# A new order for the 1,205 tasks of a block-causal attention and channel-mix kernel

## The chip, the core and the metric

The kernel runs on one core of a Trainium2 chip. The metric is the device time of one execution in microseconds (us). The kernel before the change took 271.82 us as the median of three runs (270.72 to 274.71). One further execution was taken with the hardware profiler; every time below that isn't called a median comes from it.

The core's engines run side by side, each through its own instructions in order: TensorE (PE, with its weight loads as PEld), VectorE (DVE), ScalarE (ACT), GpSimd (POOL) and SyncE (SP), whose instructions here only issue transfers. Transfers themselves are carried out by 16 DMA engines.

## What is computed

Attention over 8 batches of 8 heads, 576 positions, head size 64, with a mask by blocks of 64 positions; the result, x, with 512 columns, goes through a channel mix with squared relu and a sigmoid gate:

```python
scores = scale * np.matmul(q, k.transpose(0, 1, 3, 2))
scores = np.where(block_i >= block_j, scores, -1000000000.0)
attn = softmax(scores);  x = attn @ v            # heads side by side: 8 x 576 x 512
x_prev = x shifted by one position
xk = mu_k * x + (1.0 - mu_k) * x_prev
xr = mu_r * x + (1.0 - mu_r) * x_prev
k = np.maximum(xk @ w_k, 0.0)                    # 512 -> 1024
v = k * k @ w_v                                  # 1024 -> 512
r = 1.0 / (1.0 + np.exp(-(xr @ w_r)))            # 512 -> 512
out = r * v
```

Inputs and output are float32; the products run in bfloat16 (q, k) and float16.

## The kernel before

**Tasks.** The program makes a list of 1,205 tasks. A task is a short function that issues a few instructions of one engine. A table of numbers, `ORDER`, says in which order the tasks are issued; since every engine works through its instructions in the order of issue, the table fixes the order on each engine and in SP's queue of transfers. A number with a plus sign (`0+12`) also puts that many *spare matmuls* in front of the task (function `unread`, line 279): products of an identity matrix into a tile that nobody reads. A second table, `PLACE`, has one letter (P, D, A) for each task that may run on more than one engine: POOL, DVE or ACT.

**Buffers.** Tiles come from rings of a few buffers (line 180): 8 buffers `ld` for raw loads of q, k and weights, 4 `vl` for raw v, 4 `nb` and 8 `nl` for q and k in bfloat16, 2 `qkt` for transposed q and k, 13 `e` for exponentials, 3 `s` and 2 `mm` in PSUM. A task that takes a buffer waits until the last reader of what was there before is done. The buffer is chosen in `Plan.issue`, so a new order also gives new buffers.

**Tasks of attention**, for batch b and head pair:

- `longld` (batches 0 to 3, line 251): q or k of a head pair, rows of 2,304 bytes; `long` casts it (lines 262, 268); `qt` transposes it on PE (18 small products, line 371), `ev` copies it out of PSUM.
- `qkld` and `tlld` (batches 4 to 7, line 251): the same data in pieces of 256 bytes, two issues each; `qk` and `tail` cast it; `turn` (line 318) transposes a pair by a DMA transpose into `qkt`. In this text "turn 6 0" is that of batch 6, pair 0.
- `vld` (line 251): a piece of v; `v` casts it.
- `sc` (lines 489, 499): a group of score products; `ex` its exponential on ACT (line 517). "sc 6 01" is batch 6, group 0, block set 1; it needs the turns of pairs 0 and 2, and "sc 6 15" those of pairs 1 and 3.
- `av` S, T, A, B (lines 554, 577, 586): sums and products with v; `t1`, `rec`, `t2`, `norm` on DVE divide by the sums.

**Tasks of the channel mix**, for nine chunks c of 512 rows (batch and chunk borders differ: chunk 8 is batch 7's rows alone, chunk 7 has rows of batches 6 and 7): `d` and `mul` mix neighbouring positions (lines 739, 742, 766, 770); `pk` is xk @ w_k, eight tasks of four products each (line 794), `relu` (804, 806) and `sq` (812, 814) follow; `pr` is xr @ w_r (line 828), `tanh` follows (836); `pv` is the product with w_v, eight products (line 854), `o` combines (864), `store` writes 256 KB to the output (line 872). Weights come by `wld` (line 251) and are cast by `w`.

**What sets the order.** The core is the walk through the table:

```python
        for word in ORDER.split():
            n, _, fill = word.partition("+")
            t = self.tasks[int(n)]
            t["fill"] = int(fill or 0)
            out.append(t)
```

SP's queue holds every load, turn and store of the kernel. An instruction there that waits (a load for its buffer, a turn for its casts, a store for its output) holds all that stand behind it.

Of the kernel before, what the change touches and what calls it, by code (L numbers as in the profile page):

```python
# [14 lines left out]
LONGS = 4  # L15

ORDER = """
# [66 lines left out]
"""  # L84

PLACE = (
    "DAPAPPPPDPPDAPAPAPAPPPAPPAAADDAADDDAADDDDPPPDDPDDDDDPPPDDPPDDPPPPD"
    "PDPPPAPDAADDDDDPAPDPPAPDAAPAPADDADDADAAPPDPDPDDPDPAPPPAAADAADAAPPP"
    "ADDDDDPPADPPPDPPPDDDPPDADADDAAAPPPDDDPPPDDPPPDADPPPAPPPPDPDDPDDPDP"
    "APDDDPDAPDADADAAPDAADDDAADPADAAAPDADPDDADDPAAAADAAAAPADAAAPAPAAAAA"  # L90
    "DAAADAPAPADAPAAAAAAADAPDDAAAAAPAPAPADAAADAAAAAPADAPAAAPADDPAPADADA"
    "PAPAPADADADDAAPAPADADADADAP")


class Plan:
# [868 lines left out]
```

## Time and profile before

| | |
|---|---|
| median of three runs | 271.82 us (270.72 to 274.71) |
| profiled execution: device time | 270.97 us |
| profiled execution: span, first to last instruction | 269.2 us |
| PE busy (3,700 matmuls) | 247.1 us, 92% |
| DVE, ACT, POOL busy | 196.7, 184.8, 92.3 us |
| mean granted clock of PE | 0.987 |
| share of the 16 DMA engines that data transfers took | 75.5% |
| DMA packets under 512 bytes | 98,816 of 110,249 |
| stores after 198 us | 17 of 37 |

Device time is 1.8 us more than the span: what lies around the first and last instruction. Matmuls are pipelined, so their busy time overlaps and a busy PE isn't a PE at its peak; a group's rate is read from the starts of neighbouring groups. The share of DMA engines is that of time in which they held packets.

### The profile page before, as it was taken

The numbers are of one execution on the slowest core, as the hardware profiler recorded it, in microseconds if no ns is written. First come the engines' busy times: TensorE is split into PE (matmuls) and PEld (weight loads), VectorE is DVE, ScalarE is ACT, GpSimd is POOL, SyncE is SP. The second block draws the span as 40 slices with busy tenths as digits, with TensorE's granted clock in tenths as the row PEclk, the third lists the DMA queues.
The fourth block names the chain that finished last, engine by engine and source line by source line (L and its number), as shares of the span: only waits on it lengthen the run. The fifth ranks groups of instructions, "written<-read, shape, count | busy, mean of one in ns | idle before, by whom it ended". The sixth has DMA issues, their size and how long they took to land.

```text
span 269.2 us, 8792 instructions
## 1 busy us (share of the span) xinstructions
PE 247.1 (92%) x3700; PEld 123.4 (46%) x3700; DVE 196.7 (73%) x354; ACT 184.8 (69%) x270; POOL 92.3 (34%) x123
## 2 busy tenths in 40 slices
PE   7879779899899996789899999699999999999995
PEld 3544336444446444334354445345444544444442
DVE  1597696999888976266968969588985599943432
ACT  4869588788786885399569886695788563661440
POOL 3555614731337311365155103413403350140310
PEclk9988799999999999999999999999999999999999
DMA  7999997899999697998999899889932201202213
GB/s 217 391 205 315 268 228 209 261 259 228 220 239 223 166 226 162 207 209 225 201 198 225 195 223 207 199 192 219 194 104 78 80 4 39 80 0 79 78 56 144
DMA packets 110249, 48.83 MB, mean 181 GB/s; under 512 B 98816, under 2 KB 99072, under 8 KB 110208
## 3 DMA queue, kind: packets, MB, share of 16 engines
q1 hardware_dynamic: 110208, 48.25, 75.5%
q8 instruction: 29, 0.48, 0.8%
q14 instruction: 12, 0.10, 0.1%
HBM read 33.56 MB, written 9.44 MB: 160 GB/s over the span
## 4 chain that ended last, share of the span: by engine, by line
PE 62%; DMA 13%; DVE 8%; ACT 7%; SPq 4%; issue 3%; POOL 1%; DVEq 0%; ACTq 0%; POOLq 0%
PE t_mm L854 18%; PE t_mm L794 15%; PE t_mm L828 10%; PE t_s L489 5%; PE t_s L586 5%; DMA t_vl<-in_v_dram 4%; ACT t_e L517 4%; SPq L251 4%; DMA out_dram<-t_o 2%; DMA t_ld<-in_q_dram 2%; PE t_s L577 2%; DMA t_qkt<-t_nb 2%; PE t_s L371 2%; DMA t_ld<-in_k_dram 2%; ACT t_kr L804 2%
## 5 line engine op out<-in xcount | busy, mean ns | idle before, releaser
L517 ACT ACTIVATE t_e<-t_s 128x1024 f16<-128x1024 f32 (+1 forms) x96 | 88.9, 977 | 15.4 <-PE t_s L489 13.4
L794 PE MATMUL t_mm<-t_xk,WK 128*128 128x512 f16 x288 | 67.8, 379 | 4.1 <-ACT t_kr L804 2.7
L854 PE MATMUL t_mm<-WV,t_k 128*128 128x512 f16 (+1 forms) x296 | 66.4, 374 | 0.2 <-DVE t_k L814 0.2
L804 ACT ACTIVATE t_kr<-t_mm 128x512 f32<-128x512 f32 x61 | 36.2, 599 | 29.2 <-PE t_mm L794 23.1
L814 POOL TENSOR_TENSOR t_k<-t_kr 128x512 f16<-128x512 f32 x26 | 29.0, 1128 | 60.5 <-ACT t_kr L804 36.8
L794 PEld LDWEIGHTS <-WK 128*128 128x128 f16 x288 | 26.7, 97 | 37.0 <-issue 8.2
L854 PEld LDWEIGHTS <-t_k 128*128 128x128 f16 x296 | 27.7, 98 | 33.8 <-issue 2.3
L864 DVE SCALAR_TENSOR_TENSOR t_o<-t_t,t_mm 128x512 f32<-128x512 f32 (+1 forms) x37 | 24.8, 670 | 20.4 <-PE t_mm L854 13.0
L828 PE MATMUL t_mm<-WR,t_xr 128*128 128x512 f16 x144 | 35.9, 379 | 0.7 <-ACT t_kr L804 0.7
L770 DVE SCALAR_TENSOR_TENSOR t_xk<-t_d,MUK,t_xt 128x384 f16<-128x384 f32 (+7 forms) x56 | 30.8, 563 | 7.2 <-POOL t_d L742 7.2
L770 DVE SCALAR_TENSOR_TENSOR t_xr<-t_d,MUR,t_xt 128x384 f16<-128x384 f32 (+7 forms) x56 | 32.7, 599 | 0.0
L836 ACT ACTIVATE t_t<-t_mm 128x512 f32<-128x512 f32 x36 | 21.4, 598 | 16.1 <-PE t_mm L828 13.3
L489 PE MATMUL t_s<-t_qkt 64*64 64x64 bf16 (+7 forms) x560 | 25.4, 291 | 3.3 <-DMA t_qkt<-t_nb 3.3
L742 POOL TENSOR_TENSOR t_d<-t_xt 128x576 f32<-128x576 f32 x16 | 19.0, 1193 | 23.7 <-DVE t_xk L770 12.0
L814 DVE TENSOR_TENSOR t_k<-t_kr 128x512 f16<-128x512 f32 x24 | 18.1, 755 | 8.5 <-ACT t_kr L804 8.4
L586 PE MATMUL t_s<-t_e,t_vo 64*32 64x64 f16 (+7 forms) x1120 | 20.8, 284 | 1.1 <-POOL t_vo L268 1.1
L828 PEld LDWEIGHTS <-t_xr 128*128 128x128 f16 x144 | 13.5, 97 | 17.8 <-issue 3.0
L489 PEld LDWEIGHTS <-t_qkt 64*64 64x64 bf16 x560 | 12.4, 106 | 17.5 <-issue 10.2
L268 POOL CAST t_vo<-t_vl 128x576 f16<-128x576 f32 (+1 forms) x17 | 12.9, 761 | 20.9 <-DMA t_vl<-in_v_dram 20.9
L586 PEld LDWEIGHTS <-t_vo 64*32 64x32 f16 x1120 | 14.6, 92 | 9.1 <-issue 3.2
L268 DVE COPY t_qkt<-t_s 128x576 bf16<-128x576 bf16 x18 | 13.1, 752 | 7.3 <-PE t_s L371 6.6
L268 POOL CAST t_nl<-t_ld 128x576 bf16<-128x576 f32 x18 | 11.8, 666 | 19.0 <-DMA t_ld<-in_k_dram 13.4
(73 smaller groups left out, 242.5 us busy)
## 6 DMA issues: line engine op xcount, KB each, us to landing
out_dram<-t_o SPq DMA_DIRECT2D x35, 256.0 KB, 2.9
t_vl<-in_v_dram SPq DMA_DIRECT2D x56, 144.0 KB, 4.2
t_ld<-in_q_dram SPq DMA_DIRECT2D x16, 288.0 KB, 5.5
t_ld<-in_k_dram SPq DMA_DIRECT2D x16, 288.0 KB, 5.3
t_ld<-in_q_dram SPq DMA_DIRECT2D x32, 128.0 KB, 3.5
t_ld<-in_k_dram SPq DMA_DIRECT2D x32, 128.0 KB, 3.7
t_ld<-in_moe_w_k_dram SPq DMA_DIRECT2D x8, 256.0 KB, 6.0
t_ld<-in_moe_w_v_dram SPq DMA_DIRECT2D x8, 256.0 KB, 4.0
```

The source lines that it names most:

```text
L268: e.tensor_copy(dst, src)
L489: nc.tensor.matmul(PS[y * D:y * D + D, x, col:col + n], kq[:, 1, t * D:t * D + D], kq[:, 0, q0:q0 + n], start=True, stop=True)
L517: nc.scalar.activation(new(ebuf)[:, :, 0:w], new(m)[:, :, 0:w], AF.Exp, scale=ISQ)
L586: nc.tensor.matmul(PA[out, u, HALF + f * D:HALF + f * D + D] if kind == "T" else PA[out, u, lo - D:lo - D + n], weight((b, rows, c, t % JT ...
L770: nc.vector.scalar_tensor_tensor(dst, dt[:, 0, lo:lo + w], (MUK1, MUR1)[n][:, cc:cc + 1], x, ALU.mult, ALU.add)
L794: nc.tensor.matmul(ps, WK[:, cc, jc * P:(jc + 1) * P], new(tiles["xkb", c])[:, cc], start=(cc == 0), stop=(cc == CCn - 1))
L804: nc.scalar.activation(kt, ps, AF.Relu)
L814: (nc.vector if eng == "DVE" else nc.gpsimd).tensor_tensor(dst, KR, KR, ALU.mult)
L828: nc.tensor.matmul(ps, xr[:, cc, jt * P:(jt + 1) * P], WR[:, cc], start=(cc == 0), stop=(cc == CCn - 1))
L836: nc.scalar.activation(new(tb), new(m), AF.Tanh, scale=0.5)
L854: nc.tensor.matmul(ps[:, 0:w], k2[:, jc, jt * P:(jt + 1) * P], WV[:, jc, cols], start=(jc == 0), stop=(jc == JCn - 1))
L864: nc.vector.scalar_tensor_tensor(new(o)[:, 0:w], new(tiles["tbf", c, jt])[:, cols], 1.0, new(m)[:, 0:w], ALU.add, ALU.mult)
```

## The change

Only the two tables change. The tasks, their dependencies and the rings stay. The change's own description is: same tasks in a new order; the plan that wrote the tables now counts waits inside transfer issues, SyncE's instruction fetches, and TensorE's instruction blocks behind transfers. The planner isn't in the program; what can be seen is the new order:

```diff
 ORDER = """
-5 6 0+12 9 10 3 7 73 75 76 13 74 4 8 69+1 17 14 113 70 18 88 71 114 72 179
-81+1 89 15 83 11 181 97 98 109 12 16 84 82 110 177 178 100+4 101 182 121 122
...
+11 0+12 7 8 5 12 77 15 78 6 71 72 16 73+7 74 79 3 4 80 9 69+1 70 91 17 18 10
+13 173 174 92 75 169 76 177 178 109+4 14 113+1 88+4 110 114 89 100 97+6 85
...
 PLACE = (
-    "DAPAPPPPDPPDAPAPAPAPPPAPPAAADDAADDDAADDDDPPPDDPDDDDDPPPDDPPDDPPPPD"
...
+    "PPDDADPPPPDDDDPAPDPPPAAPADAADAADAAAADAAADDPPDDDPDDPPDDDDPDDDDDPADDP"
...
```

What differs when the tables are read out:

| | before | after |
|---|---|---|
| spare matmuls | 32 | 80 |
| last task with spares, its place in the order | `av 1 2 S`, 202 | `qt 2 0 0 1`, 195 |
| `relu` on ACT, DVE | 61, 11 | 53, 19 |
| `sq` on ACT, DVE, POOL | 22, 24, 26 | 31, 20, 21 |
| `d` on ACT, DVE, POOL | 4, 12, 16 | 4, 17, 11 |
| `qk` on ACT, DVE, POOL | 5, 15, 12 | 6, 11, 15 |
| `v` on ACT, DVE, POOL | 7, 9, 17 | 4, 13, 16 |
| first three transfers on SP | q, k of batch 0 pair 1 and q of pair 0 | q of pair 2, k of pair 0, q of pair 1 |
| `qkld` / `store` / `turn` ahead of turn 6 1 on SP | 26 / 16 / 11 | 32 / 16 / 11 |
| transfer at which the last v piece is loaded | `vld 7 1`, behind turn 7 0 | `vld 7 0`, behind turn 7 1 and three stores of chunks 4 and 5 |
| `pk` whose products PE does first | `pk 0 4` | `pk 0 0` |

The order differs on every engine from the start to the end; the number of transfers, their sizes and the products are the same.

More of the change, by code (lines that the diff above doesn't have):

```diff
@@ L17 @@
 ORDER = """
[66 rows of a table removed]
[66 rows of a table added]
 """
 PLACE = (
-    "DAPAPPPPDPPDAPAPAPAPPPAPPAAADDAADDDAADDDDPPPDDPDDDDDPPPDDPPDDPPPPD"
[L88 to L92, printed above, removed]
+    "PPDDADPPPDDDDPAPDPPPAAPADAADAADAAAADAAADDPPDDDPDDPPDDDDPDDDDDPADDP"
+    "DDAPPDPAAAADDDDPDDPPPAPPPAPDPAPDADDDAAADPPPPPADPPAPDAADADDADDDADDD"
+    "DDDPDPPDPDPPPPPDPDDADDPAPPDPDDAAPDPPPPDPDPAPPDPPDDADDPDPPAAPDDPPPP"
+    "DAPPADAADDPPAPPAPADAAAAAAADAPDPAAAADPAADPDAAPAAAADPADAAAPAPDDAAAPA"
+    "ADPADAAAPAAAAAAAPAPAPADAAAAAADPAPDAAADPDPDAADAADDDAAAAADAAADAADADA"
+    "DADADADAPAAAPADDAADADDDADDD")
 class Plan:
```

128 rows, old and new, of the table ORDER are left out of this document.

## The prediction

> **What bounds the kernel now.** I read the page's busy table first, then a table by stretch, then the chain.
>
> ```profile
> span 269.2 us, 8792 instructions
> ...
> PE 247.1 (92%) x3700; PEld 123.4 (46%) x3700; DVE 196.7 (73%) x354; ACT 184.8 (69%) x270; POOL 92.3 (34%) x123
> ...
> q1 hardware_dynamic: 110208, 48.25, 75.5%
> q8 instruction: 29, 0.48, 0.8%
> ```
>
> PE at 92% looks like the bound, but 75.5% of 16 DMA engines is 203 us, and it isn't spread evenly. The table by stretch (us; busy time and count of PE, PEld, DVE, ACT, POOL; granted clock; DMA share; GB/s) shows where:
>
> ```profile
> 18.40:21.80 3.40, 3.24 (x56) 1.71 (x55) 2.08 (x7) 2.50 (x4) 1.46 (x4) 0.50 0.94 229
> ...
> 28.70:32.10 3.40, 3.40 (x95) 1.81 (x96) 2.88 (x6) 1.33 (x2) 2.92 (x5) 0.50 1.02 221
> ...
> 42.00:60.00 18.00, 16.80 (x309) 8.78 (x302) 17.23 (x29) 14.63 (x26) 9.29 (x10) 1.00 0.83 248
> 60.00:100.00 40.00, 38.16 (x627) 19.22 (x626) 35.30 (x64) 32.04 (x47) 13.34 (x16) 1.00 1.02 217
> 100.00:170.30 70.30, 61.74 (x942) 30.24 (x940) 49.71 (x86) 49.90 (x76) 24.05 (x30) 1.00 0.98 203
> 170.30:198.00 27.70, 27.64 (x474) 13.86 (x475) 24.52 (x42) 21.51 (x32) 9.62 (x11) 1.00 0.99 211
> 198.00:269.20 71.20, 68.05 (x568) 31.89 (x566) 43.08 (x71) 35.96 (x55) 15.57 (x14) 1.00 0.16 61
> ```
>
> From 60 to 198 us the DMA engines are full (0.98 to 1.02); from 170.3 on PE doesn't pause (27.64 of 27.70, then until its last matmul at 266.05). So transfers set the pace to 170, PE after. The chain shows the handover:
>
> ```profile
> 164.27 0.63 SPq L872
> ...
> 165.02 5.30 DMA t_qkt<-t_nb
> 170.32 0.04 issue
> 170.36 0.41 PE t_s L489 x4
> ```
>
> That is turn 6 0 landing at 170.32; sc 6 01 had waited 2.1 us for it. The end is therefore: landing of the last transpose that PE waits for, plus PE's remaining work, plus 3.1 us from the last matmul to the end of the span.
>
> **Two sums, used for both orders.** First, transfers. The trace's packets by size take 21.8 ns (256 B), 97 ns (2,048 B) and 111 ns (2,304 B); over 16 engines a long load is 0.89 us, a qkld or tlld 1.40, a vld 1.57 (batch 0: 1.40, its short one 0.70), a weight or store 0.78, a turn 1.74. Added in SP's order this gives each transfer a position. The landing of each transfer in the trace minus its position is 2.0 us at 21.6 us, 4.7 at 42, 9.1 at 60, then 8.2 to 11.9 with 10.3 at turn 6 0 (position 160.0): one full stream from 60 us on, which had lost time before that. Second, PE's work: starts of neighbouring groups are 0.86 us apart for pk and pr (four 512-column matmuls, 379 ns each but pipelined), 1.73 for pv, 1.32 for av A or B, 1.36 for av S, about 0.24 for a score group, 0.22 for one spare matmul. Ahead of sc 6 01 these make 138.8, behind it 94.7; the trace took 95.7 (170.36 to 266.05).
>
> **The change, part by part.** No transfer or product is removed. (1) *Spare matmuls*, 32 become 80: 48 x 0.216 = 10.4 us of PE, the last of them in qt 2 0 0 1, where PE's sum is 36.5 us, 17.3 of it spares. I cost them at nothing: in the old order PE came to its first pk at 42.07 us with a sum of 28.0, so 14 us were idle or slow, and in the new one the sum ahead of the first pk is 37.6, which leaves 4.4 for start-up and waits to arrive as early. ACT has more ahead as well: its tasks up to batch 1's last exp come to 33.2 us by row means, 28.6 before. If that cover is gone, they delay casts, and so loads.
> The two 0.50 rows above are 6.8 us at half clock; running them at full would save PE 3.4 us. The Trainium skill (TensorE: Matmul & The Clock Gate, Part 1) says that an idle window of about 3.4 us puts the clock at half; by it the spares could win those 3.4 us of PE time, while my sum takes 0, since PE then waits for transfers anyway.
> (2) *Engine places*. By row means DVE gains about 6.7 us (8 more relus at 0.69, 5 more differences at 0.79, 4 fewer squares at 0.76 and others), ACT 1, POOL loses 12. Before, DVE was busy 67.6 of the last 98.9 us; its work behind the binding point is 63.8 us after and 66.5 before. Hidden under PE: 0.
> (3) *Order of transfers*, which decides. PE's first wait for each transpose, as position minus PE's sum ahead of it, was greatest at sc 6 01 and equal within 0.5 at the next three (sc 6 11, sc 7 15, sc 7 03): position plus work behind is 254.5 to 255.0. In the new order the greatest is at sc 6 15, which needs turn 6 1: position 171.7, PE work behind 89.1, together 260.8 (the next: sc 5 12 258.4). Ahead of it stand six more qkld (all of batch 7), two more stores and one more turn than ahead of turn 6 0 before: 6 x 1.395 + 2 x 0.776 + 1.745 = 11.7 us. PE has two pr, one pv, one av and four score groups fewer left: 1.7 + 1.7 + 1.3 + 0.9 = 5.6. With an equally full stream the end moves by 11.7 - 5.6 = **+6.0 us**.
> (4) *Waits inside the early issues*. Between 42 and 55 us SP stood still for buffers of the load ring:
>
> ```profile
> SPq L251 <- ACT t_nl L262: 2.8, 1, 2.8
> SPq L251 <- ACT WV L264: 2.0, 1, 2.0
> SPq L251 <- ACT WR L262: 1.8, 1, 1.8
> SPq L251 <- POOL t_nl L268: 1.4, 1, 1.4
> ```
>
> 8 us of standing cost the stream 4.4 (4.7 to 9.1). The new order takes loads whose buffers come free earlier against PE's non-spare work, but its spares eat part of that: the tightest loads there stand 7 to 9 us behind the PE sum they depend on, 11 to 13 before. So the gain lies between 0 and 4.4; with nothing nearer to either end I take half, **-2.2**.
> (5) *Stores in SP's queue*. A store that waits for its output holds every later load and turn. From 60 to 196 us SP's gaps between issues are 0.04 to 0.4 us, so none did. Ahead of turn 6 1 the tightest are store 3 1 0 (position 149.6, 19.3 us ahead of its PE sum) and store 2 3 0 (17.9); before, 15.7 to 16.3 at positions 69 to 88 was enough. Cost 0, up to 2 us. Behind turn 6 1 store 4 3 0 and turn 7 3 will hold SP a few us, but the later transposes have 7.6 us in hand (253.1 against 260.8).
> (6) *Instruction blocks*. PE's 29 fetches of 16 KB (q8, 0.8%) stay 29 or 30. "issue" is 3.5% of the chain, 9.4 us, fetches in it. Between 0 and 9.4 won; where PE waits for a transpose anyway it is nothing: 0.
> The Trainium skill (DMA: Bandwidth & Descriptors, Queues, rings and completion order) says that each engine takes turns between queue rows packet by packet. By that rule a fetch, on its own row, waits for a packet and not for the queued loads, and planning round it wins 0; if it did wait for the backlog, up to 9.4 us would be won. The q8 packets take 1.1 us each in the trace, against 4.2 from issue to landing for a vld, which agrees with the rule.
>
> **Sum.** Turn 6 1 lands at 170.3 + 11.7 - 2.2 = 179.8; PE's rest is 89.1 x 95.7 / 94.7 = 90.0; the tail 3.1: span 273.0, against 269.2. The profiled run took 270.97, 1.8 over its span: 274.8. The median of the runs before is 0.85 above it (271.82, runs from 270.72 to 274.71): **275.5**.
>
> **Rivals.**
> A, the forecast: 275.5, +1.4%. Chance 0.42.
> B, the stream loses nothing between 42 and 60 us, or nothing after 21 us (10.3 falls to 5.9 or even 2): 273.3 to 269.4. For: the change moves just these loads. Against: spares push PE's sum up. Chance 0.18, within 2%.
> C, slower: the spares. Casts on ACT stand behind exps that wait for PE; if PE comes to its first pk later than about 47 us (42.07 before), the load ring stays full longer than before, and each us more is one for the stream until 182 us. No gain gives 277.7; with 2 to 4 us more lost 280 to 282. For: 7 to 9 us of distance instead of 11 to 13. Against: the idle 14 us. It is the case that ends over 2% slower. Chance 0.32.
> D, the change wins what it says: PE's idle time until 170 us is fetches and blocked issues more than transfers, and their 9.4 us go: 262. For: issue's 3.5%. Against: DMA at 1.00 from 60 us. Chance 0.08, the only case over 2% faster.
>
> **Numbers.** Two per cent, 5.4 us, is about what a measurement of this kernel can tell (its runs span 4). Within 2%: A and B, 0.60; slower 0.32; faster 0.08. The range reaches from B's lower end into C's upper one, leaving out D and the worst of C: 269.5 to 281.5.
>
> **What will show it.** The new chain should hand over from a DMA on t_qkt to PE near 180 us, with PE unbroken behind it for 90 us; DMA share near 1.0 from 60 us; in 42 to 60 us a share above 0.83 (A, B) or below (C). First pk near 43 us says that the spares were covered. Half-clock rows should be fewer. I'm wrong if PE pauses after the handover for DVE or ACT, if a store holds SP ahead of turn 6 1, or if the prices per transfer change with the order.

## The result

The changed kernel takes 274.14 us as the median of 20 runs (270.00 to 278.23), the kernel before, beside it on the same chip, 271.81 (266.96 to 274.90). The ratio is **1.0136, 95% interval 1.0098 to 1.0175**: slower, by 1.4%, a difference under 2% that 20 runs tell from none. (The ratio leaves out executions that took over 1.5% more than the fastest of their kernel; the medians don't, so their quotient is smaller.) The forecast was 275.5, range 269.5 to 281.5.

The profiled execution took 274.5 us, its span 272.4; before, 270.97 and 269.2. The same lines of the page as before:

```profile
span 272.4 us, 8894 instructions
...
PE 255.1 (94%) x3748; PEld 124.8 (46%) x3748; DVE 200.1 (73%) x364; ACT 185.9 (68%) x271; POOL 83.0 (30%) x112
...
q1 hardware_dynamic: 110208, 48.25, 72.3%
q8 instruction: 29, 0.48, 0.8%
```

PE is busier by 8 us, with 48 more spare matmuls in it; the transfers are the same 110,208 packets. The table by stretch of the new kernel (busy us and count of PE, PEld, DVE, ACT, POOL; granted clock; DMA share; GB/s):

```profile
0.00:18.40 18.40, 17.01 (x207) 7.30 (x207) 5.58 (x19) 11.73 (x15) 7.12 (x22) 1.00 0.96 302
18.40:42.00 23.60, 21.95 (x500) 11.16 (x503) 18.63 (x48) 19.65 (x25) 8.18 (x13) 1.00 1.00 249
42.00:60.00 18.00, 18.00 (x472) 10.53 (x457) 17.89 (x31) 16.36 (x30) 8.79 (x11) 1.00 0.96 289
60.00:100.00 40.00, 37.87 (x579) 18.53 (x579) 32.90 (x60) 30.37 (x44) 15.49 (x19) 1.00 0.91 217
100.00:170.30 70.30, 63.79 (x985) 31.35 (x985) 54.92 (x94) 50.63 (x74) 26.68 (x30) 0.98 0.99 205
170.30:182.00 11.70, 9.18 (x125) 4.11 (x123) 7.99 (x15) 7.03 (x11) 3.09 (x5) 1.00 0.61 127
182.00:198.00 16.00, 16.00 (x244) 7.82 (x243) 13.24 (x23) 11.72 (x17) 3.89 (x4) 1.00 0.93 186
```

Two readings carry the rest. In 42 to 60 us the DMA engines now have a share of 0.96, where it was 0.83: the stream loses under 1 us there (landing minus position), where it lost 4.4. SP's waits (41 to 61 us) are shorter, not gone: 7.9 us in all, the longest 1.6, against 9.7 and 2.8. And PE's last pause, in 170.30:182.00, ends at 177.68, 7.3 us later than the old kernel's (170.36); from there on PE is unbroken. From 60 to 100 us the share is 0.91, not near 1.0 as forecast, while 217 GB/s move as before, when it was 1.02: a share near 1 by itself doesn't say that no more could be moved.

The chain of the new kernel at that place (start, us, what):

```profile
171.65 4.16 DMA t_ld<-in_q_dram
...
176.02 0.06 POOL t_nb L268
176.07 0.51 issue
176.59 1.05 POOL t_k L814
...
177.68 1.25 PE t_mm L854 x5
178.94 0.86 PE t_mm L828 x4
179.80 0.62 PE t_s L489 x20
```

The handover to PE is not a DMA on `t_qkt`, as forecast. It is qkld 7 1 0 landing, its cast on POOL, then a square on POOL, then pv 4 3 0 on PE. Turn 6 1 had landed at 177.98; PE came to sc 6 15, which needs it, only at 179.89, 1.9 us later. POOL's timeline in the new kernel (start, busy; in brackets the idle time ahead and what ended it) shows the square waiting behind a cast that had nothing to cast yet:

```profile
168.81 1.35 POOL L742 TENSOR_TENSOR t_d<-t_xt 128x576 f32<-128x576 f32 x1
176.02 0.61 POOL L268 CAST t_nb<-t_ld 128x512 bf16<-128x512 f32 x1 [5.86 <-DMA t_ld<-in_q_dram]
176.59 1.04 POOL L814 TENSOR_TENSOR t_k<-t_kr 128x512 f16<-128x512 f32 x1
```

### The profile page after: what moved, and what is told of

The parts are those of the page before. It is cut to its first block, busy times and chain, and to the rows that moved or that the text cites. A ratio compares the mean times of both kernels' runs of the same rounds, so it can differ in the third digit from the quotient of the medians.

```text
span 272.4 us, 8894 instructions
## 1 busy us (share of the span) xinstructions
PE 255.1 (94%) x3748; PEld 124.8 (46%) x3748; DVE 200.1 (73%) x364; ACT 185.9 (68%) x271; POOL 83.0 (30%) x112
## 2 busy tenths in 40 slices
DMA packets 110248, 48.82 MB, mean 179 GB/s; under 512 B 98816, under 2 KB 99072, under 8 KB 110208
## 3 DMA queue, kind: packets, MB, share of 16 engines
q1 hardware_dynamic: 110208, 48.25, 72.3%
## 4 chain that ended last, share of the span: by engine, by line
PE 69%; DVE 15%; DMA 8%; issue 3%; POOL 1%; ACT 1%; SPq 1%; POOLq 0%; DVEq 0%; ACTq 0%
PE t_mm L794 19%; PE t_mm L854 17%; PE t_mm L828 8%; PE t_mm L279 6%; PE t_s L586 5%; PE t_s L489 5%; DMA t_qkt<-t_nb 3%; PE t_s L577 3%; DMA t_ld<-in_q_dram 3%; DVE t_xr L770 3%; PE t_s L371 2%; DVE t_xk L770 2%; DVE t_d L742 2%; DVE t_xt L650 2%; DVE t_o L864 2%
## 5 line engine op out<-in xcount | busy, mean ns | idle before, releaser
L804 ACT ACTIVATE t_kr<-t_mm 128x512 f32<-128x512 f32 x53 | 31.6, 599 | 25.5 <-PE t_mm L794 25.5
L814 POOL TENSOR_TENSOR t_k<-t_kr 128x512 f16<-128x512 f32 x21 | 22.8, 1093 | 52.1 <-ACT t_kr L804 42.3
L770 DVE SCALAR_TENSOR_TENSOR t_xk<-t_d,MUK,t_xt 128x384 f16<-128x384 f32 (+7 forms) x56 | 33.3, 609 | 1.8 <-POOL t_d L742 1.7
L489 PE MATMUL t_s<-t_qkt 64*64 64x512 bf16 (+7 forms) x560 | 25.3, 291 | 5.2 <-DMA t_qkt<-t_nb 5.2
L742 POOL TENSOR_TENSOR t_d<-t_xt 128x576 f32<-128x576 f32 x11 | 13.3, 1213 | 42.5 <-DVE t_xt L642 20.6
L812 ACT ACTIVATE t_k<-t_kr 128x512 f16<-128x512 f32 x31 | 18.7, 635 | 6.5 <-PE t_mm L854 4.5
L806 DVE TENSOR_SCALAR t_kr<-t_mm 128x512 f32<-128x512 f32 x19 | 12.9, 686 | 13.0 <-PE t_mm L794 7.4
L586 PE MATMUL t_s<-t_e,t_vo 64*32 64x512 f16 (+7 forms) x1120 | 21.1, 294 | 0.0
L650 DVE TENSOR_TENSOR t_xt<-t_s,t_rt 128x1024 f32<-128x1024 f32 x14 | 17.1, 1218 | 4.3 <-PE t_s L586 4.0
L279 PE MATMUL t_mm<-identb 128*128 128x512 bf16 x62 | 18.5, 426 | 1.4 <-POOL identb masks.py:199 1.4
```

Source lines behind the costliest of these rows:

```text
L279: nc.tensor.matmul(spare.get("at", dst), identb, identb[:, :].unsqueeze(1).to_broadcast([P, 4, P]), start=True, stop=True)
L489: nc.tensor.matmul(PS[y * D:y * D + D, x, col:col + n], kq[:, 1, t * D:t * D + D], kq[:, 0, q0:q0 + n], start=True, stop=True)
L586: nc.tensor.matmul(PA[out, u, HALF + f * D:HALF + f * D + D] if kind == "T" else PA[out, u, lo - D:lo - D + n], weight((b, rows, c, t % JT ...
L650: nc.vector.tensor_tensor(xt[:, :, 1 + D:1 + S].rearrange("p (u f) t -> p f u t", f=2)[:, "AB".index(kind)], new(m[kind]), rt_[:, :, D:S], ...
L770: nc.vector.scalar_tensor_tensor(dst, dt[:, 0, lo:lo + w], (MUK1, MUR1)[n][:, cc:cc + 1], x, ALU.mult, ALU.add)
L804: nc.scalar.activation(kt, ps, AF.Relu)
```

## The experiments

Twelve kernels, each compared with the kernel before on the same chip. A span in the table is that of one execution, and executions of one kernel differ by 4 us and more, so a difference of 1 to 3 us between two spans shows nothing by itself. Three theories were weighed. **Theory 1** is that of the prediction: a full stream of transfers in SP's order, and PE's work behind the transpose it waits for last. **Theory 2** is that the spares cost the time. **Theory 3** came from the chain above: casts of late loads, at the head of POOL's or DVE's queue, hold what PE needs. All edits are in `Plan.order`, unless told otherwise; moves that the programs spell out one by one are written as a loop.

| kernel | median us | ratio, 95% interval | profiled span us |
|---|---|---|---|
| new, as changed | 274.14 | 1.0136, 1.0098 to 1.0175 | 272.4 |
| new without spares | 273.76 | 1.0107, 1.0064 to 1.0150 | 269.6 |
| old with late loads | 278.88 | 1.0270, 1.0201 to 1.0339 | 278.5 |
| early new, late old | 276.30 | 1.0205, 1.0138 to 1.0272 | 273.0 |
| early old, late new | 280.91 | 1.0380, 1.0330 to 1.0431 | 279.0 |
| old with thin stores | 265.77 | 0.9820, 0.9765 to 0.9875 | 263.8 |
| new with thin stores | 269.52 | 0.9953, 0.9916 to 0.9990 | 267.2 |
| new, cast behind square | 273.60 | 1.0074, 1.0028 to 1.0120 | 273.8 |
| new, turn earlier, cast later | 273.91 | 1.0063, 1.0017 to 1.0110 | 273.3 |
| new, three casts later | 272.97 | 1.0101, 1.0037 to 1.0165 | 271.1 |
| new, late part rearranged | 274.04 | 1.0124, 1.0078 to 1.0170 | 272.2 |
| new, rearranged from 250 | 274.16 | 1.0146, 1.0088 to 1.0204 | 272.1 |
| old, rearranged from 120 | 279.20 | 1.0316, 1.0244 to 1.0387 | 275.0 |

### The spares alone

```diff
-        for word in ORDER.split():
+        words = ORDER.split()
+        words = [w if w == "0+12" else w.partition("+")[0] for w in words]
+        for word in words:
```

> The changed kernel with only the 12 spares ahead of the first task; the other 68 unread products are left out, and nothing that the output needs. Theory 1: TensorE comes to its first pk up to 10 us earlier and waits as much longer for transposes; turn 6 1 lands within 1 us of 178.0; the time is 0 to 1 us under the changed kernel's, ratio to the old one 1.005 to 1.009; there may be more half-clock stretches before 60 us. Theory 2 (spares cost): 68 x 0.216 = 14.7 us less TensorE work, and the time falls by 2.3 us or more, to the old kernel's or below, ratio 1.00 or less.

The ratio is 1.0107 against 1.0136 with spares, intervals overlapping: taking 68 spares (14.7 us of PE by their price) out wins 0.3%, which the intervals don't tell from nothing. Theory 2 falls, since it needs 1.00 or less and the interval starts at 1.0064. The table by stretch of the kernel without spares, first 60 us:

```profile
0.00:18.40 18.40, 13.24 (x218) 7.07 (x218) 4.77 (x17) 11.38 (x14) 7.05 (x22) 0.84 0.97 295
18.40:42.00 23.60, 16.51 (x493) 11.70 (x495) 21.11 (x50) 21.07 (x27) 8.10 (x13) 0.79 1.00 251
42.00:60.00 18.00, 16.85 (x394) 9.61 (x391) 17.27 (x31) 14.33 (x27) 8.42 (x11) 0.96 0.99 298
```

The DMA share is as high as with spares (0.97, 1.00, 0.99), so the early stream belongs to the order and not to the spares. What goes is the granted clock, to 0.84 and 0.79, at no cost that shows in the time. If each PE group is priced as in the prediction and subtracted from the time to the next group's start, PE loses 22.9 us up to 60 us without the spares and 7.8 with them: 15.1 against the 14.7 that the spares take. They fill holes to within half a microsecond. (The profiled span without them, 269.6, is 2.8 us shorter than with them; the medians don't bear that out. In this execution turn 6 1 was issued at 170.90 us, 2.4 us sooner than with spares, and PE did sc 6 15 at 176.28: a landing within 1 us of 178.0, as expected, it was not.)

### The price of late transfers, alone in the old order

Six transfers are moved from behind turn 6 0 (task 636) to ahead of it, in the old order:

```diff
+        words = ORDER.split()
+        for w in ("733", "731", "739", "719", "661", "972"):
+            words.remove(w)
+            words.insert(words.index("636"), w)
```

> The old order, with six transfers (qkld 7 2 1, 7 2 0, 7 3 1 and 7 0 0, vld 6 3, store 3 0 0) moved from just behind turn 6 0 to just ahead of it; nothing else moves. Theory 1 (the two sums): turn 6 0 goes from position 160.0 to 167.9, the greatest sum of position and PE work behind from 255.1 to 262.8, so +7.7 us: ratio 1.028, with turn 6 0 landing near 178 us and PE unbroken behind sc 6 01. Rival (the transfers near 170 us are hidden, and the loss of the new order lies earlier): the same time, ratio 1.00 to 1.01. More than 1.035 would say that the moved loads wait for buffers and hold SP.

The ratio is 1.027 against 1.028 expected. The chain, and then the waits of PE between 160 and 190 us (us in total, times, longest), of this kernel (its lines stand 13 later: L502 is sc, L331 turn, L264 a load):

```profile
173.82 4.45 DMA t_qkt<-t_nb
178.27 0.04 issue
178.31 0.64 PE t_s L502 x4
```

```profile
PE t_s L502 <- DMA t_qkt<-t_nb: 7.9, 1, 7.9
```

Turn 6 0 landed at 178.27 ("near 178"), its landing minus position still 10.35, as in the old kernel (10.3). So a transfer moved ahead of the binding transpose does cost its full price, and the 11.7 us that step 3 of the prediction puts on the moved transfers is of the right kind and size. That is shown in the old order; whether moving transfers back wins it in the new one is asked further down. The span grew by 9.3 us, 1.6 more than the price. Most of that is the clock behind the 7.9 us of idle time. In the table by stretch, the first row has the wait in it, and the second is what comes right behind it:

```profile
170.30:182.00 11.70, 3.82 (x89) 1.79 (x88) 4.94 (x6) 2.01 (x4) 2.36 (x3) 0.71 0.95 204
178.30:181.70 3.40, 3.39 (x84) 1.75 (x88) 3.35 (x4) 1.51 (x2) 2.36 (x3) 0.51 1.03 201
```

From the handover to the last matmul (275.44) PE took 97.1 us here and 95.7 in the old kernel. There the pause ahead of the handover was 2.1 us and the clock stayed at 1.00. The Trainium skill (TensorE: Matmul & The Clock Gate, Part 1) puts the idle window that halves the clock at about 3.4 us; a pause of 2.1 with, and one of 7.9 without, a full clock behind it agree with that. Another trace goes further: in the kernel "new, late part rearranged" a pause of 2.1 us from 111.7 us on was also followed by 3.4 us at half clock (0.50 from 114.24 to 117.65), PE having been busy for 1.15 of the 3.24 us before. So a pause need not fill such a window.

### Old and new order joined

The first 322 tasks of the new order (to longld 3 0 1 1, with the new spares and places), then the others in the old order; and the first 348 of the old (to longld 3 1 1 0), then the others in the new:

```diff
+        words = ORDER.split()
+        words = words[:words.index("365") + 1]    # "371" in the other
+        done = {int(w.partition("+")[0]) for w in words}
+        words += [w for w in ORDER2.split()
+                  if int(w.partition("+")[0]) not in done]
```

> The new order up to its transfer longld 3 0 1 1 (its first 322 tasks, all 80 spares among them), then the tasks that are left in the order and on the engines of the old one. Theory 1 (the two sums: the transfer stream, which both orders keep full after 60 us, and TensorE's work behind the last awaited transpose): the early part keeps the 4 us that it won in the stream and the late part goes back to position plus work of 255.0, so the end comes 4 us before the old kernel's: span near 265.2, time near 267.7, ratio to the old kernel 0.985. Theory 2 (the 48 more spares are what the change costs, 10.4 us of TensorE early on, part of it covered): all spares are still there, so the time stays near the changed kernel's 274.1, ratio 1.009.

> The other half: the old order up to its transfer longld 3 1 1 0 (348 tasks, 32 spares), then what is left in the new order and on its engines. Theory 1: position plus work is 260.8 as in the changed kernel and the stream has lost its 4 us between 42 and 60 us, so turn 6 1 lands near 182 and the end comes 6 us after the old kernel's: span near 275, time near 277.6, ratio 1.021. Theory 2 (spares): none of the new ones is there, so the time is that of the old kernel or less, ratio 1.00 or below.

Both were meant to separate step 3 (late, +6.0) from step 4 (early, -4 as it came out), and both lost more than either theory says: 276.3 where theory 1 said 267.7, and 280.9 where it said 277.6. The loss lies at the joint. What SP waited for between 60 and 165 us in the first, new then old (lines stand 82 later: L954 is a store, L946 the `o` ahead of it):

```profile
SPq L954 <- DVE t_o L946: 4.4, 1, 4.4
...
SPq L954 <- DVE t_xr L852: 2.4, 1, 2.4
```

Two stores held SP's queue for 6.8 us, and the DMA share from 60 to 100 us was 0.80 (0.91 in the new kernel, 1.02 in the old one). Landing minus position, 5.3 at 48 us, was 11.6 at turn 6 0: the early gain had been given back ahead of the handover. What PE waited for between 60 and 100 us in the second, old then new (L453 is `qt`, L350 a cast):

```profile
PE t_s L453 <- POOL t_nl L350: 9.1, 2, 5.0
```

Casts came late on POOL, and the clock fell to 0.79 there. Landing minus position was 13.0 at turn 6 1, which landed at 184.64, 6.7 us later than in the new kernel; the span is 6.6 longer. So the joined kernels don't give the price of one half alone, and that the early part is worth 4 us and the late one 6 is not shown by them. In the second, PE came to sc 6 15 at 186.48, 1.8 us behind the turn's landing, after 1.5 us of waiting for a square on POOL: the same queue as in the new kernel, moved by as much as the stream was late.

### Less to transfer

Every store writes only 64 of its columns; the rest of the output is left out.

```diff
-                nc.sync.dma_start(o2[g:g + P, cols], new(o)[:, 0:w])
+                thin = slice(cols.start, cols.start + 64)
+                nc.sync.dma_start(o2[g:g + P, thin], new(o)[:, 0:64])
```

> The old order; every store writes only 64 of its columns, so most of the output is left out and a store's rows are 256 bytes: by the packet prices 0.17 us of the stream instead of 0.78. Nothing else changes. Theory 1: 14 stores stand ahead of turn 6 0, its position falls by 8.4, the greatest sum from 255.1 to 246.4: -8.7 us, ratio 0.968. Rival (PE's own waits for the other engines set the time as much as transfers): about half or less of that, ratio 0.985 to 1.00.

> The new order with the same thin stores (64 of the columns written, the rest of the output left out). Theory 1: 16 stores stand ahead of turn 6 1, the greatest sum falls from 260.8 to 251.2: -9.6 us against the new kernel, about 264.5 us, ratio to the kernel before 0.976. Rival (waits inside the core, such as PE's for POOL, hold it): 270 us or more, ratio 0.995 or more.

In both orders some 5 us of the 9 came. The old kernel went to 0.982 (0.968 expected), its turn 6 0 landed 5.0 us earlier (165.32) where the position says 8.4, and the span fell by 5.4. The new one went to 0.9953 (0.976 expected), turn 6 1 4.7 earlier (173.26), span 5.2 shorter. So what the stream wins at this transpose is won at the end, about one for one, but the stream doesn't win all that it no longer carries. In the old order PE waits for the transpose (1.6 us at sc 6 01); in the new one it came to sc 6 15 only 0.8 us behind the landing, so there the equal size is no proof that this transpose binds, and the ratio is the one that the rival named (0.995 or more). From 60 to 165 us the tables by stretch of the two thin kernels, old and then new, are:

```profile
60.00:165.00 105.00, 98.61 (x1565) 49.26 (x1564) 83.56 (x150) 81.80 (x121) 38.59 (x46) 1.00 0.90 186
```

```profile
60.00:165.00 105.00, 100.12 (x1607) 49.21 (x1592) 87.71 (x151) 80.62 (x117) 41.15 (x47) 1.00 0.91 185
```

The DMA share is 0.90 and 0.91, with whole stores 0.99 and 0.96: something else held the stream. That SP now waits longer for buffers and casts is not shown: its named waits in this stretch are 14.2 us in the old order (15.7 with whole stores) and 18.4 in the new (18.0). A rival that no run here tests is SP itself. Of these 105 us it spends 95.9 inside its transfer instructions, waits included, with thin stores and 95.8 with whole ones (old order), and issuing a thin store takes it as long as a whole one (median 0.42 and 0.43 us). If SP's own pace is nearly as tight a limit as the DMA engines, a lighter store can't win its whole price. Between the two thin kernels the new order is still slower, by 3.75 us.

### Casts that stand in front

First the POOL cast behind the square:

```diff
+        words.remove("726")                               # qk 7 1 0
+        words.insert(words.index("993") + 1, "726")       # sq 4 3
```

> The changed kernel with one task moved on GpSimd: the cast of qkld 7 1 0 (task 726) behind the square sq 4 3 (993) instead of ahead of it. In the changed kernel's trace GpSimd waits 5.9 us for that load, the square ends at 177.63 and pv 4 3 0 stands for 2.7 us. Theory 1 with this queue as the last 2 us: pv 4 3 0 runs through, TensorE comes to sc 6 15 near 177.4 and waits for turn 6 1 until 178.0, and the end comes 2 us earlier: time near 272.1, ratio 1.001. If the stretch is hidden anyway (another wait takes its place), the time stays at 274.1, ratio 1.009, and the trace shows TensorE waiting past 179 us for something else.

The wait at pv 4 3 0 went, and another came, in the waits of PE from 170 to 190 us (L857 is pv, L867 is `o`):

```profile
PE t_mm L857 <- DVE t_o L867: 1.7, 1, 1.7
```

This is pv 4 0 0: it needs the PSUM buffer that o 4 3 0 empties, and on DVE that stood behind the cast of qkld 7 0 0. DVE's timeline has that cast:

```profile
177.63 0.82 DVE L271 CAST t_nb<-t_ld 128x512 bf16<-128x512 f32 x1 [1.97 <-DMA t_qkt<-t_nb]
```

Its load had landed at 176.36; what it waited for is turn 6 1, which landed at 177.50 and until then read the `nb` buffer that the cast writes. In the new kernel the cast had waited 2.6 us there too, for the same turn. So the turn still held PE, by way of a buffer and DVE's queue. The ratio, 1.0074, is 0.6% below that of the new order, about as much as the two intervals leave open. Then the same cast with turn 6 1 moved forward:

```diff
+        words.remove("642")                               # turn 6 1
+        words.insert(words.index("981"), "642")           # store 3 3 0
```

> The new order with two moves: turn 6 1 ahead of store 3 3 0 (position 171.7 to 165), and the cast of qkld 7 1 0 behind the square sq 4 3 on POOL. Theory 1: the greatest sum falls from 260.8 to 258.5 (now sc 5 12 with turn 5 3, and sc 6 15 with turn 6 3 at 258.0), -2.3 us, and the 1.9 us by which PE came late to sc 6 15 go too: 270 to 272 us, ratio 0.995 to 1.002. Rival (what PE waits for near 175 to 180 us is the chain through DVE, ACT and POOL, and another link takes the place of the one removed): 273 to 274 us, ratio 1.007 to 1.010, as with the second move alone.

Turn 6 1 landed at 169.30 instead of 177.98, 8.7 us earlier, and nothing was won over the cast alone: 1.0063. PE waited 3.3 us at pv 4 0 0, until o 4 3 0 had run behind the same DVE cast, which this time waited for its load (qkld 7 0 0 landed at 177.11 here, behind the turn). So at this place the binding transfer of the new order isn't turn 6 1 alone: the loads of batch 7 just ahead of it hold PE equally, through queues. The price of step 3 is not won back by moving this one transfer. Last, all three casts moved back, with the transfers where they were:

```diff
+        for w, a in (("726", "993"),                      # qk 7 1 0, sq 4 3
+                     ("720", "1024"), ("729", "1024")):   # o 4 3 0
+            words.remove(w)
+            words.insert(words.index(a) + 1, w)
```

> The new order with three casts moved behind the work that stood behind them: qk 7 1 0 behind the square sq 4 3 on POOL, qk 7 0 0 and tail 7 1 behind o 4 3 0 on DVE; the transfers stay. With the first move alone PE waited 1.7 us at pv 4 0 0, which needs the PSUM buffer that o 4 3 0 empties, and o 4 3 0 stood behind the cast of qkld 7 0 0 on DVE. Theory 3 (casts that wait for late loads at the head of a queue are what holds PE near 178 us): that wait goes too, PE runs through at turn 6 1's landing, about 1.5 us less than with the first move alone: 272 us, ratio 1.000 to 1.004. Rival (turn 6 1 itself, or another link, holds PE as long): 273.5, ratio 1.007 to 1.010.

The waits of PE from 140 to 200 us are now:

```profile
PE t_s L496 <- DMA t_qkt<-t_nb: 2.3, 1, 2.3
PE t_mm L861 <- POOL t_k L821: 0.2, 1, 0.2
```

The 2.3 is at sc 5 12 near 148 us; in 170.30:182.00 PE is busy all 11.70. The waits that theory 3 names are gone, and the span is 271.1 instead of 272.4. In the times a gain isn't shown: 1.0101, with an interval from 1.0037 to 1.0165 that holds the rival's expectation and just reaches theory 3's. What these waits are worth stays open between nothing and some 3 us.

### Orders with smaller sums

If the two sums were all, an order with a smaller greatest sum would be faster. The tasks behind a certain one were rearranged, by moving single tasks and keeping what shortened the end in a small model: engines in order, rings, one stream of transfers, prices from the rows. Engine places, spares and tasks ahead are unchanged. The core of the first, from the 600th task:

```diff
-922 486 432 510 565 910 501 481 450 499 440 495 911 441 567 932 923 500 924
+452 910 479 451 565 432 450 507 643 560 440 508 922 923 442 546 510 924 443
...
```

that of the second, from the 250th, and of the third, in the old table from the 120th:

```diff
-814 188 275 54 300 299 48 166 49 191 808 65 66 297 67 815 816 192 821 822 50
+808 240 54 166 377 59 275 167 297 48 815 814 60 816 191 457 458 829 49 300
...
-1 134 135 274 170 231 232 266 221 136 96 174 229 195+2 222 193 108 105 276
+120 229 35 223 170 134 135 230 108 96 224 137 105 140 1 2 154 221 222 193
...
```

> The new order up to its 600th task, with all its engine places and spares; the other 605 tasks are rearranged among themselves so that the greatest sum of position and PE work falls from 260.8 to 254.0 (turns 5 3, 6 2, 6 3 and 6 1 stand earlier against PE's work) and no cast that waits for a late load stands ahead of work that PE needs soon. Theory 1 with theory 3: 6.8 us less than the new order, 267 us, ratio 0.986. Rival (waits inside the core come back elsewhere, as with the thin stores, where half of the gain came): 270.7 us, ratio 0.998.

> The same from the 250th task on: greatest sum 251.4. Theory 1 with theory 3: 9.4 us less than the new order, 264.7 us, ratio 0.977; with half of it 269.4 us, ratio 0.994. If the rearranged tasks of 45 to 95 us put the load ring out of step, as in the two orders joined from old and new, the stream loses 2 to 5 us there and the ratio is near 1.

> The old order up to its 120th task, with its engine places and 32 spares; the others rearranged in the same way: greatest sum 251.4 instead of 255.1. Theory 1 with the old landing minus position (10.3) at the binding transpose: -3.7 us, ratio 0.986; with the 4 us of the early stream won as well, -8 us, ratio 0.971. Rival (only the new order's engine places and spares bring the early stream, and the late part keeps its inner waits): ratio 0.995 to 1.005.

None is shown to be faster than the new kernel, and all are slower than the old one. The first came to 1.0124 (0.986 expected), the second to 1.0146 (0.977), the third to 1.0316 (0.986 or 0.971). The transposes moved as meant: in the first, turn 6 1 landed at 163.42 and turn 6 3 at 166.15, and no transfer held PE from 130 to 182 us. But the time is the same. The waits of PE from 182 to 262 us in it (L827 is pr, L793 pk, L863 `o`, L805 relu):

```profile
PE t_mm L827 <- DVE t_o L863: 1.3, 1, 1.3
PE t_mm L793 <- DVE t_kr L805: 0.7, 1, 0.7
```

In the new kernel PE waits for nothing in that stretch. PE's time over its work, by stretch, adds it up (us; each group priced as in the prediction):

| | to 60 | 60 to 100 | 100 to 170 | 170 to 198 | from 198 | sum |
|---|---|---|---|---|---|---|
| old | 16.2 | 4.0 | 11.6 | 1.1 | 0.4 | 33.5 |
| new | 7.8 | 4.2 | 10.5 | 3.5 | 0.3 | 26.3 |
| new, late part rearranged | 8.6 | 2.9 | 8.6 | 2.7 | 3.2 | 26.1 |
| new, rearranged from 250 | 9.9 | 4.3 | 7.3 | 2.2 | 2.0 | 25.7 |
| old, rearranged from 120 | 19.5 | 8.8 | 5.4 | 3.0 | 2.4 | 39.0 |

(Rows may differ from their sum by 0.2.) From 100 to 170 us the rearranged orders win 2 to 6 us, as the sums say in sign, and lose it again: the first behind 198 us (2.9), the second before 100 (2.2) and behind 198 (1.7), the third before 100 (8.1) and behind 170 (3.9). The behaviour of the end, "no pause behind the handover", was a property of those two orders, and it goes when others shorten the wait ahead of it. Why the small losses add up so is not settled beyond the waits named; the two sums lack what makes them.

## Why the prediction came out right

By its steps:

- **Spares, 0**: right, shown by the kernel without them. The clock's half-speed rows are gone (1.00 up to 60 us), as the rule of the Trainium skill (TensorE: Matmul & The Clock Gate, Part 1) on idle windows would have it, and the 3.4 us of PE that this could win did not show in the time, as the sum had it. First pk at 44.56 us instead of 43.
- **Engine places, 0**: right for the busy time (DVE +3.4 us, POOL -9.3, where row means gave +6.7 and -12), but wrong for the queues. sq 4 3 and the cast of qkld 7 1 0 were both on DVE; the change puts both on POOL, the square right behind the cast, and the wait for that late load becomes PE's. No busy time shows that.
- **Order of transfers, +6.0**: the price of a transfer moved ahead holds, by the six transfers moved in the old order (7.7 expected, 7.95 at the landing, ratio 1.027). That it is the cause of the new order's 1.4% is the account of the trace, not of an experiment: moving turn 6 1 ahead of other transfers again, or rearranging for smaller sums, did not bring the old time back.
- **Early waits, -2.2**: mis-sized. Turn 6 1's landing minus position is 6.3, before it was 10.3 at turn 6 0: 4.0 us came instead of 2.2, which is what rival B described. (It was 4.3 to 4.6 near 97 us and grew again to 6.3; by what is not shown.) The half was taken for want of a nearer row. The spares, feared to delay early casts and loads, did not: landing minus position at turns 4 0 and 4 2, near 97 us, lies between 4.3 and 4.6 with them and without.
- **Stores, 0**: right ahead of turn 6 1. Behind it, store 4 3 0 and turn 7 3 did hold SP (issues at 180.2 and 184.9 us), at no cost. That stores can hold SP for longer was seen at the joint of the early new, late old kernel.
- **Instruction blocks, 0**: 29 fetches before and after, 0.8% both. No run separates their cost. The prediction sets the 1.1 us that a fetch's packets take against a load's 4.2 us from issue to landing; but a packet's own time doesn't tell how long it stood in line, so this bears little on the rule it is put beside.
- **Handover**: forecast at 179.8 by turn 6 1; it landed at 177.98, and PE got there at 179.89. The missing step is the queue: qkld 7 1 0 is one of the six more qkld that step 3 counted as stream time, but it also released a cast in front of work that PE needed. So -1.8 in step 4 and +1.9 in the missing step cancel, and that the handover time is right to 0.1 us is luck. Two of the prediction's own signs did not come: the handover from a DMA on `t_qkt`, and the DMA share near 1.0 from 60 us on (0.91 to 100 us).
- **Behind it**: 179.89 to the last matmul at 269.29 is 89.4 (90.0 forecast), then 3.1: span 272.4 against 273.0, device time 274.5 against 274.8. The median of more runs lies 0.4 below the profiled run, not above it, which is most of the 1.4 us by which the forecast was too high. (Its own last step, 274.8 and 0.85, gives 275.6 and not 275.5.)

Rival C (spares) and D (idle time of fetches and issues) fall: the first by the run without spares, the second by the time: the early stream did lose less, and "issue" is still 3.1% of the chain (3.5% before), but the kernel got slower. What B said of the stream happened; what A said of the end happened, since the queue took the difference.

## What to carry to other kernels

When transfers pace one part and an engine the rest, find the handover, then ask for each moved transfer on which side of it it stands: moved ahead, it can cost its full price at the end (7.7 us expected and 7.95 measured here); moved back, it wins nothing as long as another transfer holds the same place. Then look at what the late transfers release: a cast at the head of an in-order queue makes everything behind it wait for that transfer, whatever the queue's busy share. And take a sum of this kind as a price of single moves, not as a goal to minimise: three orders with smaller sums were not faster, and what took the difference was found only in part.

## What the runs showed of the hardware that was not expected

- A long wait is paid twice. Behind 7.9 us of PE idle the granted clock was 0.51 for 3.4 us, and the rest of PE's work took 1.4 us more than behind a 2.1 us wait with a clock of 1.00; two waits of 9.1 us together, the longest 5.0, put 60 to 100 us at 0.79.
- A low clock where PE has idle time anyway need not cost: 0.84, 0.79 and 0.96 over the first 60 us against 1.00 made no difference that can be told in 272 us.
- Rows of 256 bytes instead of 2,048 in the stores took eight times less data, and the trace's packet prices (21.8 and 97 ns) 4.5 times less of the stream; a little over half of what that saves ahead of the handover reached the end, 1.8% of the time in both orders.
